# Three pairs' normalising products from VectorE to GpSimd, with a reordered broadcast and reordered weight pieces

## The chip, the core and the metric

The kernel runs on one core of a Trainium2 chip. The core has TensorE (PE in the profile; PEld is its weight load), VectorE (DVE), ScalarE (ACT), GpSimd (POOL) and SyncE (SP), which here only issues DMAs. Each engine works off its own queue in order and waits for the others through semaphores. The metric is the device time of one execution in microseconds; lower is better.

## What is computed

Attention over 4 batches of 8 heads with 576 tokens and 64 numbers per head, then a convolutional gated feed-forward layer on the joined heads:

```python
q_rot, k_rot = rotate(q), rotate(k)            # rotary embedding
scores = 1/sqrt(64) * q_rot @ k_rot.T
scores = scores - max(scores, axis=-1)
attn = exp(scores)
attn = attn / (sum(attn, axis=-1) + 1e-09)     # the normalising factor
x = (attn @ v) -> (B, 576, 512)
h = maximum(x @ w_in, 0)                       # 512 -> 1024
conv_out = 3-tap depthwise convolution of h along the tokens
out = (h * sigmoid(conv_out)) @ w_out          # 1024 -> 512
```

The weights arrive as 64-bit floats and are turned into 32-bit ones on the chip.

## The kernel before

Two heads make a pair; there are 16 pairs, four to a batch, and each takes 5 steps of the plan: pair p has its first scores in step 5p. A step holds one block of 128 query rows: scores on TensorE into PSUM (`sp`, line 259 and 285), the row maxima on VectorE (`negm`, line 267), the exponentials on ScalarE (`st`, line 271), the turning of the exponentials on TensorE (`tp`, line 319), their evacuation on ScalarE (`pt`, line 198). Five steps later the pair's product with v is made on TensorE (`emit_E`, line 396) and put into `xn` by ScalarE (line 406).

The order is written out by hand: `at(n, rank, fn)` puts a piece of work into step n, and within a step the lower rank comes first. Each engine's queue is what this order leaves on it. The steps below 26 (`WIDE`) are the first part: the pairs 0 to 5 start there and the weights are converted in between. From step 26 on TensorE also does the feed-forward layer (first matmul in line 453 for batch 0, line 463 for the others, second in line 575 and 555), and PSUM and SBUF are shared out anew.

What the change touches:

- **Rope.** GpSimd rotates q and k (lines 189 and 192, six products and three sums for each of q and k) in the raw tiles `rq` and `rk`, of which there is one each. The q of pair 4 is rotated in step 14, of pair 5 in step 19, of pair 6 in step 24, each followed by its k. VectorE then turns `rq` into `qT` (line 232) and `rk` into `kT` (line 235); only after that can SP load the next pair's q or k.
- **The normalising factor.** `emit_rinv` (VectorE, line 365 to 367) makes the reciprocals of the sums; SP writes them to DRAM (`rd`, line 370), and `emit_rb` loads them back spread over the partitions with three DMAs (`rb`, lines 376 to 378). There is one `rb` buffer: the next pair's broadcast has to wait for this pair's last product.
- **The product.** `norm` (line 414) multiplies `xn` by `rb`, two halves per pair. For batch 0 (pairs 0 to 3) the result goes to `xr`, which the first feed-forward matmul reads in step 26 and after. The steps of the two halves are 10 and 11 for pair 0, 15 and 16 for pair 1, 20 and 21 for pair 2, 24 and 25 for pair 3.
- **Weight pieces.** `WPIECES` lists 16 pieces of 128 rows and 512 columns (or the like). The first 12 are converted in the first part: an Abs on ScalarE (line 602), four operations on VectorE (lines 605, 611, 616, 621). A piece of w_in ends there, as `wr`. A piece of w_out lands in a scratch tile `wf`, ScalarE rounds it to `wouth` (line 688), and GpSimd takes the rest in four subtractions (`woutl`, line 685). In the list the eight pieces of w_in come first, then four of w_out.

The scratch tiles `wf` lie in memory that is given back at step 26; the convolution's `c` tiles (line 478, ScalarE) come to lie there.

Of the kernel before, what the change touches and what calls it, by code (L numbers as in the profile page):

```python
# [12 lines left out]
ALU = mybir.AluOpType  # L13
# [7 lines left out]
def attention_moe_kernel(ctx, tc, q, k, v, w_in, conv_w, w_out, tab, tabx, out):  # L21
    nc = tc.nc
# [5 lines left out]
    NK = DM // 128  # L28
    NF = DFF // 128
    HS = S // 2  # L30
    XW = HS + 2
# [341 lines left out]
    def emit_rb(p):  # L373
        fl = rds.pop(p).rearrange("(o t) n -> o (t n)", o=1)
        rbt = rb[p] = p1.tile([128, S], F32, tag="rb", name="rb")
        nc.sync.dma_start(out=rbt[0:64, :], in_=fl[:, 0:S].to_broadcast([64, S]))
        nc.sync.dma_start(out=rbt[64:128, 0:512], in_=fl[:, 640:1152].to_broadcast([64, 512]))
        nc.sync.dma_start(out=rbt[64:128, 512:S], in_=fl[:, 576:640].to_broadcast([64, 64]))
# [11 lines left out]
    def emit_E(p, j, a=0, n=XW):  # L390
        b, hp = divmod(p, NPB)
        xp = m_tile()[:, 0:n] if "m" in psum else spare(n)
        o = (S - XW) * j
        for i in range(5):
            for h in range(2):
                nc.tensor.matmul(  # L396
                    out=xp[64 * h:64 * h + 64, :],
                    lhsT=vmain[p][:, h, i, :] if i < 4 else vrem[p % 2][:, h, :],
                    rhs=pt[:, 2 * i + h if i < 4 else 8, o + a:o + a + n],
                    start=(i == 0),  # L400
                    stop=(i == 4),
                )
        if a == 0:
            xns[p, j] = p2.tile([128, XW], F32, tag="xn", name="xn", bufs=4)
        xn = xns[p, j]
        after(lambda: nc.scalar.activation(out=xn[:, a:a + n], in_=xp, func=AF.Copy))

        def norm():
            if plain(2 * b):
                dst = xraw[hp, j] = xtra.tile([128, XW], F32, tag="x", name="xr")  # L410
            else:
                xslot[b, hp, j] = free_slots.pop(0)
                dst = xn
            nc.vector.tensor_tensor(out=dst, in0=xn, in1=rb[p][:, o:o + XW], op=ALU.mult)

        def high():
            nc.scalar.activation(out=x_at(xslot[b, hp, j], 0), in_=xn, func=AF.Copy)  # L417

        def low():
            sl = xslot[b, hp, j]  # L420
            nc.gpsimd.tensor_tensor(out=x_at(sl, 1), in0=xn, in1=x_at(sl, 0).bitcast(F32), op=ALU.subtract)  # L421

        def both():
            norm()
            if not plain(2 * b):
                defer(1, lambda: (high(), low()))

        norms[p, j] = both
# [198 lines left out]
    def bits(i):  # L627
# [2 lines left out]
        return struct.unpack("<f", struct.pack("<I", i))[0]  # L630

    stage = {}
    WPIECES = [(w_in, None, None, kk, 1, c) for c in (0, 512) for kk in range(NK)] + [
        (w_out, wouth, woutl, f, 1, 0) for f in range(NF // 2)
    ] + [(w_out, wouth, woutl, f, 2, c) for c in (0, 256) for f in range(NF // 2, NF, 2)]

    def load_w(i):
        src, _, _, kk, rows, c = WPIECES[i]
# [107 lines left out]
    def at(n, rank, fn):  # L746
        plan.setdefault(n, []).append((rank, len(plan.get(n, [])), fn))

    def emit():
        with tc.manual_schedule(engines=engines):  # L750
# [34 lines left out]
            for p in range(NP):  # L785
                n = STEPS * p
                for s in range(STEPS):
                    m = n + s
                    first = m < WIDE
                    if m:  # L790
                        at(m - 1 if first else m, 0.5 if first else 0, lambda p=p, s=s: emit_S(p, s))
                    at(m, 0.2, lambda p=p, s=s: go(reds, (p, s)))
                    at(m, 0.3 if first else 1.5, lambda p=p, s=s: go(exps, (p, s)))
                    for h in range(2 if s < 4 else 1):
                        at(m + 1, 0 if m + 1 < WIDE else 1, lambda p=p, s=s, h=h: emit_T(p, s, h))
                if n + 4 < WIDE:
                    for i in range(4):
                        at(n + 1 + i, 2, lambda p=p, i=i: emit_Trem(p, i))
                else:
                    for i in range(4):  # L800
                        at(n + 1 + i, 1.1, lambda p=p, i=i: emit_Trem(p, i))
                if n + 8 < WIDE:
                    for i in range(4):
                        at(n + 5 + i, 4, lambda p=p, i=i: emit_E(p, i // 2, XW // 2 * (i % 2), XW // 2))
                else:
                    for i in range(2):
                        m = n + 5 + (i if n + 5 < WIDE else 0)
                        at(m, 4 if m < WIDE else 10, lambda p=p, i=i: emit_E(p, i))
                at(n + 5, 4.5, lambda p=p: emit_rinv(p))
                at(n + 5 + (n + 8 < WIDE), 17 if n + 8 < WIDE else 4.6, lambda p=p: emit_rb(p))  # L810
                for j in range(2):
                    at(n + NORM.get(p, 8 if n + 8 < WIDE else 7) + (j if p <= WIDE // STEPS else 0), 1.7 + j, lambda p=p, j=j: norms.pop((p, j))())
            whole, done = sum(c for c, _ in wsteps), 0
            for i, (c, u) in enumerate(wsteps):
                at(1 + int((WIDE - 2) * done / whole) if i else 0, 0.4, u)
# [105 lines left out]
```

## Time and profile before

| what | us |
|---|---|
| median of 3 runs | 473.69 (473.57 to 474.65) |
| the profiled execution | 474.58 |
| its span (first to last instruction) | 472.8 |
| TensorE busy | 456.9 (97%) |
| VectorE busy | 352.8 (75%) |
| ScalarE busy | 327.8 (69%) |
| GpSimd busy | 292.6 (62%) |

A row of the timeline has the start and the length of a group of equal instructions in microseconds from the span's start, the engine, the line, the operation with its tiles (out<-in), how many they are, and in brackets how long the engine stood idle before them and what ended that. A row by stretch has the busy time of each engine in that stretch, with the number of instructions. The granted TensorE clock is at its upper level in every stretch.

### The profile page before, as it was taken

Reading aid. Unit: us, or ns where it says so; the run is one execution under the profiler, and the core shown is the slowest. Engines: PE = TensorE matmul, PEld = TensorE weight load, DVE = VectorE, ACT = ScalarE, POOL = GpSimd, SP = SyncE. Lnnn points to the kernel's source line nnn. Section 1 sums busy time; section 2 is a strip of 40 time slices with the busy share of each in tenths; the row PEclk is TensorE's granted clock in tenths of the full one; section 3 lists DMA queues with packets and bytes.
Section 4 is the critical chain, followed back from the end, with each engine's and each line's share of the span. In section 5 each row is a group of like instructions: output and inputs, shape, how many; then the busy total and the mean of one; then the engine's idle time right before and its main releaser. Section 6 shows DMA issues by size and latency. Waiting matters only on the chain.

```text
span 472.8 us, 12261 instructions
## 1 busy us (share of the span) xinstructions
PE 456.9 (97%) x4563; PEld 358.2 (76%) x4563; DVE 352.8 (75%) x642; ACT 327.8 (69%) x942; POOL 292.6 (62%) x474
## 2 busy tenths in 40 slices
PE   8789999899999999999999999999999999999997
PEld 8355666556666877778787979888797878899886
DVE  4799999976999897678687786866765747468921
ACT  2789889887898877869596868868686854244400
POOL 2967884998689796997939392929430332243610
PEclk9999999999999999999999999999999999999999
DMA  9898778363571714126161717143010000100011
GB/s 230 202 214 198 161 176 191 91 155 72 121 150 50 138 37 100 40 58 118 38 139 38 139 37 134 41 90 88 27 49 28 24 27 0 46 23 24 0 68 44
DMA packets 103695, 42.63 MB, mean 90 GB/s; under 512 B 94524, under 2 KB 97876, under 8 KB 103636
## 3 DMA queue, kind: packets, MB, share of 16 engines
q1 hardware_dynamic: 103184, 41.50, 38.4%
q8 instruction: 36, 0.59, 0.5%
q10 hardware_dynamic: 452, 0.35, 0.2%
q14 instruction: 23, 0.19, 0.1%
HBM read 37.04 MB, written 4.79 MB: 88 GB/s over the span
## 4 chain that ended last, share of the span: by engine, by line
PE 76%; DVE 7%; ACT 7%; POOL 5%; DMA 2%; issue 1%; SPq 0%; DVEq 0%; POOLq 0%; ACTq 0%
PE sp L259 12%; PE pm L396 11%; PE mt L555 11%; PE pm L575 10%; PE pm L463 9%; PE mt L463 7%; PE tp L319 6%; PE pm L453 5%; ACT st L271 3%; DVE negm L267 3%; PE sp L396 2%; POOL rk L189 2%; ACT pt L198 2%; PE tp L764 1%; POOL woutl L685 1%
## 5 line engine op out<-in xcount | busy, mean ns | idle before, releaser
L267 DVE TENSOR_REDUCE negm<-sp 128x1 f32<-128x576 f32 x144 | 102.4, 747 | 27.7 <-PE sp L259 20.1
L271 ACT ACTIVATE st<-sp,negm 128x576 f32<-128x576 f32 x128 | 94.0, 742 | 26.6 <-DVE negm L267 22.4
L259 PE MATMUL sp<-kT,qT 64*128 64x288 f32 (+4 forms) x556 | 94.2, 449 | 0.7 <-ACT kT L198 0.7
L198 ACT ACTIVATE pt<-tp 128x512 f32<-128x512 f32 (+3 forms) x176 | 84.7, 535 | 4.4 <-PE tp L319 3.8
L484 DVE SCALAR_TENSOR_TENSOR c<-rr,cw,c 128x288 f32<-128x288 f32 x128 | 78.9, 616 | 4.2
L502 POOL TENSOR_TENSOR gm<-c,gm 128x288 fp32r<-128x288 f32 (+4 forms) x72 | 46.1, 645 | 48.9 <-ACT gm L501 48.7
L189 POOL TENSOR_TENSOR rq<-rq,tabt 128x192 f32<-128x192 f32 x90 | 59.6, 695 | 18.5 <-DMA rq<-q 14.3
L189 POOL TENSOR_TENSOR rk<-rk,tabt 128x192 f32<-128x192 f32 x90 | 59.1, 689 | 7.3 <-DMA rk<-k 5.4
L259 PEld LDWEIGHTS sp<-kT,qT 64*128 64x128 f32 (+1 forms) x556 | 44.4, 174 | 22.6 <-issue 9.8
L319 PEld LDWEIGHTS tp<-idf,st 64*128 64x128 f32 x1024 | 41.3, 138 | 21.3 <-ACT st L271 9.2
L319 PE MATMUL tp<-idf,st 64*128 64x64 f32 x1024 | 47.2, 226 | 5.9 <-ACT st L271 5.2
L396 PE MATMUL pm<-pt,vm 128*64 128x290 f32 x368 | 49.7, 411 | 0.2 <-ACT pt L198 0.2
L575 PE MATMUL pm<-wouth,gm 64*128 64x256 f32 x512 | 49.6, 284 | 0.0
L493 DVE SCALAR_TENSOR_TENSOR c<-c,rr 128x288 f32<-128x288 f32 x64 | 37.6, 608 | 9.5 <-ACT c L490 9.3
L482 DVE TENSOR_SCALAR c<-rr,cw 128x288 f32<-128x288 f32 x56 | 24.4, 436 | 22.7 <-ACT rr L474 22.4
L575 PEld LDWEIGHTS pm<-wouth,gm 64*128 64x128 f32 x512 | 41.0, 185 | 0.0
L421 POOL TENSOR_TENSOR xT<-xn,xT 128x290 fp32r<-128x290 f32 x18 | 15.8, 877 | 37.1 <-ACT xT L417 37.1
L396 PEld LDWEIGHTS pm<-pt,vm 128*64 128x64 f32 x368 | 25.5, 136 | 17.4 <-ACT pt L198 0.6
L463 PE MATMUL pm<-xT,wh 128*128 128x290 f32 x176 | 37.0, 302 | 0.0
L575 PE MATMUL pm<-woutl,gm 64*128 64x256 f32 x256 | 36.4, 278 | 0.0
L490 ACT ACTIVATE c<-c 128x288 f32<-128x288 f32 x64 | 28.4, 444 | 11.4 <-DVE c L484 11.4
L453 PE MATMUL pm<-xr,wr 128*128 128x290 f32 x128 | 34.5, 417 | 0.0
(135 smaller groups left out, 974.9 us busy)
## 6 DMA issues: line engine op xcount, KB each, us to landing
rq<-q SPq DMA_DIRECT2D x60, 144.0 KB
rk<-k SPq DMA_DIRECT2D x60, 144.0 KB
w<-moe_w_in SPq DMA_DIRECT2D x8, 512.0 KB
vm<-v SPq DMA_DIRECT2D x32, 128.0 KB
rb<-rd SPq DMA_DIRECT2D x16, 144.0 KB
out<-oh SPq DMA_DIRECT2D x18, 128.0 KB
rb<-rd SPq DMA_DIRECT2D x16, 128.0 KB
w<-moe_w_out SPq DMA_DIRECT2D x4, 512.0 KB
```

What stands on the lines that cost most here:

```text
L189: nc.gpsimd.tensor_tensor(out=y, in0=y, in1=tabt[:, a:a + 3], op=ALU.mult)
L198: nc.scalar.activation(out=out, in_=in_, func=AF.Copy, scale=1.0 if sc is None else sc)
L259: nc.tensor.matmul(out=out, lhsT=qt[64 * h:64 * h + 64, c], rhs=kt[64 * h:64 * h + 64, a:a + n], start=True, stop=True)
L267: reds.setdefault((p, s), []).append(lambda: nc.vector.tensor_reduce(out=nm, in_=sc, axis=AX.XY if len(sc.shape) == 3 else AX.X, op=ALU.ma ...
L271: lambda: nc.scalar.activation(out=dst, in_=sc, func=AF.Exp, bias=nm, scale=1.0, accum_out=sm)
L319: nc.tensor.transpose(ps[r][:, 64 * k:64 * k + 64], x[i], idf[i, i])
L396: nc.tensor.matmul(out=xp[64 * h:64 * h + 64, :], lhsT=vmain[p][:, h, i, :] if i < 4 else vrem[p % 2][:, h, :], rhs=pt[:, 2 * i + h if i < ...
L453: nc.tensor.matmul(out=ps[:, 0:XW], lhsT=raws[kk, half][:, gs], rhs=xraw[kk, j], start=(kk == 0), stop=(kk == NK - 1))
L463: nc.tensor.matmul(out=ps[:, 0:XW], lhsT=w, rhs=x_at(xs, e), start=(i == 0), stop=(i == n - 1))
L484: nc.vector.scalar_tensor_tensor(out=c, in0=r[:, j + e:j + e + HS], scalar=cw[:, 8 * e + f:8 * e + f + 1], in1=c, op0=ALU.mult, op1=ALU.add,)
L555: nc.tensor.matmul(out=ops[tt][:, 0:width], lhsT=g_tile(tt, f, e), rhs=w[:, f, cols], start=(f == 0 and i == 0), stop=(f == NF - 1 and i = ...
L575: nc.tensor.matmul(out=ps[r][:, 0:256], lhsT=g_tile(tt, f, e)[rows], rhs=w[rows, f, cols], start=(f == 0 and i == 0), stop=(f == NF - 1 an ...
```

## The change

The products of pairs 0, 1 and 2 (line 414, now 415) are made by GpSimd in place of VectorE. Pair 3's products stay on VectorE; its second one goes from step 25 to step 26. In step 21 pair 3's broadcast gets rank 15 in place of 17, so that SP issues it ahead of pair 6's q, which has rank 16. In `WPIECES` the four early pieces of w_out come between the two halves of w_in.

```diff
-            nc.vector.tensor_tensor(out=dst, in0=xn, in1=rb[p][:, o:o + XW], op=ALU.mult)
+            eng = nc.gpsimd if p < 3 else nc.vector
+            eng.tensor_tensor(out=dst, in0=xn, in1=rb[p][:, o:o + XW], op=ALU.mult)
...
-    WPIECES = [(w_in, None, None, kk, 1, c) for c in (0, 512) for kk in range(NK)] + [
+    WPIECES = [(w_in, None, None, kk, 1, 0) for kk in range(NK)] + [
         (w_out, wouth, woutl, f, 1, 0) for f in range(NF // 2)
-    ] + [(w_out, wouth, woutl, f, 2, c) for c in (0, 256) for f in range(NF // 2, NF, 2)]
+    ] + [(w_in, None, None, kk, 1, 512) for kk in range(NK)] + [(w_out, wouth, woutl, f, 2, c) for c in (0, 256) for f in range(NF // 2, NF, 2)]
...
-                at(n + 5 + (n + 8 < WIDE), 17 if n + 8 < WIDE else 4.6, lambda p=p: emit_rb(p))
+                at(n + 5 + (n + 8 < WIDE), 15 if n + 10 == WIDE - 1 else 17 if n + 8 < WIDE else 4.6, lambda p=p: emit_rb(p))
                 for j in range(2):
-                    at(n + NORM.get(p, 8 if n + 8 < WIDE else 7) + (j if p <= WIDE // STEPS else 0), 1.7 + j, lambda p=p, j=j: norms.pop((p, j))())
+                    at(n + NORM.get(p, 8 if n + 8 < WIDE else 7) + (2 * j if n + 10 == WIDE - 1 else j if p <= WIDE // STEPS else 0), 1.7 + j, lambda p=p, j=j: norms.pop((p, j))())
```

GpSimd's queue before, from pair 4's q to pair 6's k (`rq`, `rk` are the ropes, `woutl` the subtractions):

```order
L189 TENSOR_TENSOR rq<-rq,tabt 128x192 x6
L192 TENSOR_TENSOR rq<-rq 128x6x32 x3
L189 TENSOR_TENSOR rk<-rk,tabt 128x192 x6
L192 TENSOR_TENSOR rk<-rk 128x6x32 x3
L685 TENSOR_TENSOR woutl<-wf,wouth 128x128 x4
L189 TENSOR_TENSOR rq<-rq,tabt 128x192 x6
L192 TENSOR_TENSOR rq<-rq 128x6x32 x3
L189 TENSOR_TENSOR rk<-rk,tabt 128x192 x6
L192 TENSOR_TENSOR rk<-rk 128x6x32 x3
L685 TENSOR_TENSOR woutl<-wf,wouth 128x128 x8
L189 TENSOR_TENSOR rq<-rq,tabt 128x192 x6
```

GpSimd's queue now, from the end of pair 3's k to the end of pair 5's k and the two products behind it:

```order
L415 TENSOR_TENSOR xr<-xn,rb 128x290
L686 TENSOR_TENSOR woutl<-wf,wouth 128x128 x4
L415 TENSOR_TENSOR xr<-xn,rb 128x290
L686 TENSOR_TENSOR woutl<-wf,wouth 128x128 x4
L189 TENSOR_TENSOR rq<-rq,tabt 128x192 x6
...
L192 TENSOR_TENSOR rk<-rk 128x6x32 x3
L686 TENSOR_TENSOR woutl<-wf,wouth 128x128 x4
L415 TENSOR_TENSOR xr<-xn,rb 128x290 x2
L686 TENSOR_TENSOR woutl<-wf,wouth 128x128 x4
...
L192 TENSOR_TENSOR rk<-rk 128x6x32 x3
L415 TENSOR_TENSOR xr<-xn,rb 128x290 x2
```

Two products and eight subtractions now stand between pair 3's k and pair 4's q, as many between pair 4's k and pair 5's q, and pair 2's two products behind pair 5's k; the subtractions behind pairs 5 and 6 are gone.

VectorE's queue now, from the first row after pair 5's `kT` (step 24) to step 27:

```order
L267 TENSOR_REDUCE negm<-sp 128x1
L622 SCALAR_TENSOR_TENSOR wr<-w_1073,wt 128x512
L415 TENSOR_TENSOR xr<-xn,rb 128x290
L267 TENSOR_REDUCE negm<-sp 128x1 x2
L365 SCALAR_TENSOR_TENSOR rvc_85<-sums 128x9
...
L267 TENSOR_REDUCE negm<-sp 128x1 x2
L606 TENSOR_SCALAR room<-room 128x512
L612 TENSOR_SCALAR room<-room 128x512
L232 STREAM_TRANSPOSE qT<-rq 128x576
L415 TENSOR_TENSOR xr<-xn,rb 128x290
L267 TENSOR_REDUCE negm<-sp 128x1 x2
```

Before, pair 3's second product stood right behind the two maxima of step 25; now it stands behind pair 6's `qT`, and the first one still stands ahead of step 25's maxima.

SP's queue now, the piece of pair 3's broadcast and pair 6's q:

```order
L370 DMA rd<-rt 9x32 x4
L376 DMA rb<-rd 64x576
L377 DMA rb<-rd 64x512
L378 DMA rb<-rd 64x64
L150 DMA rq<-q 32x18x64 x4
L645 DMA room<-moe_w_out 128x2x256
L150 DMA rk<-k 32x18x64 x4
```

Before, the four loads of `rq` stood ahead of the three of `rb`. The first of a broadcast's three DMAs waits for the last reader of the `rb` buffer, which for the broadcasts of pairs 1, 2 and 3 was VectorE and is now GpSimd.

## Rows read from the trace of the kernel before

**Rows 1.** Busy time of each engine by stretch (us; instructions), clock, DMA.
```profile
82.10:99.90 17.80, 15.52 (x190) 10.16 (x188) 17.55 (x31) 14.88 (x42) 17.80 (x29) 1.00 0.52 129
99.90:111.00 11.10, 10.32 (x95) 6.91 (x91) 5.42 (x15) 6.76 (x19) 9.72 (x18) 1.00 0.58 144
111.00:130.00 19.00, 19.00 (x164) 12.97 (x164) 17.07 (x31) 17.04 (x49) 13.63 (x22) 1.00 0.33 75
...
150.00:381.00 231.00, 230.33 (x2675) 188.17 (x2673) 171.53 (x312) 177.08 (x517) 149.54 (x247) 1.00 0.32 70
```

**Rows 2.** Tile rb: VectorE's products of pairs 0 to 3 (ns min/median/max).
```profile
L414 DVE TENSOR_TENSOR xr<-xn,rb x8: 454/705/855, 48.1 to 98.8; 128x290 f32<-128x290 f32 x8
```

**Rows 3.** Timeline of VectorE: maxima of step 22, pair 5's kT and what follows.
```profile
88.89 1.41 DVE L267 TENSOR_REDUCE negm<-sp 128x1 f32<-128x576 f32 x2
...
94.28 0.76 DVE L235 STREAM_TRANSPOSE kT<-rk 128x576 f32<-128x576 f32 x1
...
96.85 0.71 DVE L414 TENSOR_TENSOR xr<-xn,rb 128x290 f32<-128x290 f32 x1
97.49 1.41 DVE L267 TENSOR_REDUCE negm<-sp 128x1 f32<-128x576 f32 x2
```

**Rows 4.** Timeline of ScalarE: exponentials of steps 22 and 25, and a tap.
```profile
90.33 0.74 ACT L271 ACTIVATE st<-sp,negm 128x576 f32<-128x576 f32 x1 [1.76 <-DVE negm L267]
...
99.90 0.74 ACT L271 ACTIVATE st<-sp,negm 128x576 f32<-128x576 f32 x1
...
109.65 0.53 ACT L478 ACTIVATE c<-rr,cw 128x288 f32<-128x288 f32 x1 [3.41 <-POOL woutl L685]
```

**Rows 5.** Timeline of TensorE: turning after step 22's exponentials; steps 26 and 27.
```profile
91.94 0.46 PE L319 MATMUL tp<-idf,st 64*128 64x64 f32 x8 [0.26 <-ACT st L271]
...
103.40 2.22 PE L453 MATMUL pm<-xr,wr 128*128 128x290 f32 x8
...
110.65 0.39 PE L356 MATMUL pm<-idf,st 64*128 64x64 f32 x2 [0.78 <-ACT pt L198]
```

**Rows 6.** Timeline of GpSimd from pair 3's k to the last early subtractions.
```profile
55.07 2.32 POOL L192 TENSOR_TENSOR rk<-rk 128x192 f32<-128x192 f32 x3
59.34 3.80 POOL L189 TENSOR_TENSOR rq<-rq,tabt 128x192 f32<-128x192 f32 x6 [1.95 <-DVE wt L616]
...
66.14 3.87 POOL L189 TENSOR_TENSOR rk<-rk,tabt 128x192 f32<-128x192 f32 x6 [1.18 <-DVE wt L616]
69.97 1.90 POOL L192 TENSOR_TENSOR rk<-rk 128x192 f32<-128x192 f32 x3
78.07 2.48 POOL L685 TENSOR_TENSOR woutl<-wf,wouth 128x128 fp32r<-128x128 f32 x4 [6.20 <-ACT wouth L688]
80.51 4.01 POOL L189 TENSOR_TENSOR rq<-rq,tabt 128x192 f32<-128x192 f32 x6
...
90.47 2.14 POOL L192 TENSOR_TENSOR rk<-rk 128x192 f32<-128x192 f32 x3
92.57 4.68 POOL L685 TENSOR_TENSOR woutl<-wf,wouth 128x128 fp32r<-128x128 f32 x8
...
107.92 1.70 POOL L685 TENSOR_TENSOR woutl<-wf,wouth 128x128 fp32r<-128x128 f32 x4
```

**Rows 7.** Groups of GpSimd by form: subtractions as large as a product (busy us, mean ns).
```profile
L421 POOL TENSOR_TENSOR xT<-xn,xT 128x290 fp32r<-128x290 f32 x18 | 15.8, 877 | 37.1 <-ACT xT L417 37.1
```

**Rows 8.** Timeline of SP: broadcasts of pairs 3 and 5.
```profile
90.59 0.46 SPq L376 DMA_DIRECT2D rb<-rd  x1
...
91.73 0.60 SPq L378 DMA_DIRECT2D rb<-rd  x1
...
131.35 0.46 SPq L376 DMA_DIRECT2D rb<-rd  x1
```

**Rows 9.** Timeline of VectorE: the product that waited for pair 5's broadcast.
```profile
136.40 0.47 DVE L414 TENSOR_TENSOR xn<-xn,rb 128x290 f32<-128x290 f32 x1 [0.92 <-DMA rb<-rd]
```

**Rows 10.** Chain that ended last, in order of time (start, us): a load of q.
```profile
89.92 2.97 DMA rq<-q
```

## Prediction

> **What bounds the kernel now.** First the busy time by stretch [rows 1]. From 111 us on TensorE has no gap worth naming: 19.00 of 19.00 us, and 230.33 of 231 us between 150 and 381. In that part a change can gain only by letting TensorE begin sooner. Up to 100 us it is otherwise: in the last stretch of the first part VectorE is busy 17.55 and GpSimd 17.80 of 17.80 us, and TensorE 15.52. Between 99.9 and 111 us TensorE lacks 0.78 us. The rows show that loss as one wait: at 110.65 it waits 0.78 us for ScalarE [rows 5], which itself stood 3.41 us in a tap (line 478) until the last early subtraction of GpSimd was done at 109.62 [rows 4]. So the question is how much sooner TensorE's first feed-forward matmul (103.40, [rows 5]) comes, and whether the 0.78 us goes.
>
> **What the change removes.** (1) Six of VectorE's eight products of batch 0, with a median of 0.705 us [rows 2]: 6 x 0.705 = 4.2 us of VectorE. What of it lies on the path is seen where ScalarE waits for the maxima: 1.76 us ahead of the exponentials of step 22 [rows 4], which follow the maxima at 88.89 [rows 3] at once. I take 1.76 us as the most that TensorE can be ahead at step 25 by this term.
> (2) The tap's wait. Its `c` tile lies where a scratch tile of a w_out piece was, and the last piece converted is now one of w_in, which GpSimd does not touch. So no wait on GpSimd is left there, and TensorE's 0.78 us goes. Ahead of the tap's new place ScalarE has time: it waits anyhow for TensorE's product with v. I count the 0.78 us whole; at worst it is 0.
>
> **What it adds.** GpSimd gets six products. The trace has none of them on GpSimd; the nearest row is its subtraction of the same 128x290, 0.877 us on average [rows 7]. From below I take VectorE's own shortest, 0.454 us [rows 2], as no row shows GpSimd the faster of the two; from above 1.28 us, the average stretched as four subtractions beside a busy VectorE were against the last four (2.48/1.70 = 1.46, [rows 6]). I take 0.88, the row of equal shape. The Trainium skill's GPSIMD Engine Reference (4.1 Engine selection) speaks against the change: a product of two inputs belongs on VectorE, being about half as fast on GpSimd. The ratio 0.877/0.454 = 1.9 agrees with it.
>
> **The queue behind them.** GpSimd works in order, so the ropes of pairs 4 and 5 stand behind the products and the moved subtractions. Pair 3's k ends at 55.07 + 2.32 = 57.39 [rows 6], and nothing of the change lies ahead of it on GpSimd. From there the new order is:
> - two products and eight subtractions: 2 x 0.88 + 4.68 (the eight at 92.57, [rows 6]) = 6.44
> - pair 4's rope: from 59.34 to 69.97 + 1.90 = 71.87, less the wait of 1.18 inside [rows 6]: 11.35
> - again two products and eight subtractions: 6.44
> - pair 5's rope: from 80.51 to 90.47 + 2.14 = 92.61 [rows 6]: 12.10
>
> 57.39 + 6.44 + 11.35 + 6.44 + 12.10 = 93.72 us, against 92.61 before. GpSimd's waits of before (1.95, 1.18 and 6.20 us, [rows 6]) pay for nearly all of the added work, but they are used up. Pair 5's `kT` was made at 94.28 [rows 3], so the maxima of step 24 are still at about their old time or a little ahead. SP is held on the way too: the broadcast of pair 1 until pair 0's second product (57.39 + 2 x 0.88 + half of 4.68 = 61.5), that of pair 2 until about 75.18 + 2.34 + 1.76 = 79.3. Behind them stand pair 4's and pair 5's k. With some 2 us for the issues ahead and 5.05 us to land (below) these are there at 69 and 86; GpSimd comes to them at 69.4 and 87.5, half a rope after 63.83 and 81.62. So this costs nothing, though by little.
>
> **The wait that is added.** Behind pair 5's k stand pair 2's two products, which end at 93.72 + 1.76 = 95.48. Only then may SP issue pair 3's broadcast, because the one `rb` buffer is read by them; before it went out at 90.59 [rows 8]. Behind it on SP are queued pair 6's q, a weight piece, pair 6's k, v of pair 5. From the first DMA of a broadcast to its product there is one row in which the product waited for it: 131.35 to 136.40, 5.05 us [rows 8, 9]. From below: the third DMA is issued 91.73 - 90.59 = 1.14 us after the first [rows 8], and a load of q took 2.97 us from issue to its release [rows 10], together 4.11. I take 4.6, the middle. The Trainium skill's page DMA: Bandwidth & Descriptors (Anatomy of one DMA) gives a fixed 2.0 us and bytes over 436 GB/s; for the 0.13 MB of the second DMA that is an estimate of 2.3 us, so 1.14 + 2.3 = 3.4 in all. By that page the sum below would end 1.2 us lower, at 472.4; the rows are longer, and I keep to them.
>
> So pair 3's first product can start on VectorE at 95.48 + 4.6 = 100.08; before it started at 96.85 [rows 3]. It stands ahead of the maxima of step 25, and the whole score path stands behind it: product 0.45 (no GpSimd work is then ready, so the shortest of [rows 2]), both maxima 1.41 [rows 3], done at 101.94. The first exponential waits for both (88.89 + 1.41 = 90.30 and 90.33, [rows 3, 4]), so step 25's start at about 101.97; they were at 99.90 [rows 4]. The second head's turning on TensorE came 91.94 - 90.33 = 1.61 us after the first exponential's start [rows 4, 5], now 103.58; it takes 0.46 [rows 5], and the first feed-forward matmul follows at about 104.1, against 103.40: **0.7 us later**. VectorE's 1.76 us of term (1) are gone in this wait. With the 0.78 us of term (2) TensorE is 0.1 us ahead from step 27 on.
>
> The other edits: pair 3's second product leaves step 25 and waits with `qT` of pair 6 in step 26. Pair 6's q is loaded behind the broadcast, about 97.2 to 99.3, is there at about 102, and its rope ends about 107.3 (5.3 us: pair 6's q and k ran from 92.57 + 4.68 = 97.25 to 107.92, [rows 6]); the maxima behind it need step 27's scores, which TensorE makes at 108 or later. That cover is thin: each us that the rope of pair 6 is later than 108 is one of TensorE. The w_out pieces' rounding on ScalarE comes earlier by the same count; ScalarE has 14.88 of 17.80 us in the last stretch, from which it is taken away [rows 1]. Both cost nothing where they stand.
>
> The sum: 4.2 us leave VectorE, of them 1.76 could be gained; the late broadcast takes these and 0.7 more; 0.78 comes from the tap. against the profiled execution (474.58, of which 1.78 lie outside the span of 472.8 and are not touched) that makes 474.5; the median of the runs, 473.69, lies 0.9 below it, so the forecast is **473.6 us**.
>
> **Rivals.**
> (A) *The broadcast comes in time.* The sum stands on 95.48 - 57.39 = 38.1 us of unbroken GpSimd work, and its rows were measured while VectorE also made the products that now leave it. Without these, and with VectorE waiting for the ropes, GpSimd may run faster: the last four subtractions took 1.70 where four took 2.48 under load [rows 6]. From 1.3 us saved on (3%) the gain is over 0.3%; from 2.5 us on (7%) product and broadcast no longer hold up VectorE, and the 1.76 us stay: 473.69 - 1.76 - 0.78 = 471.2. Against it: in the stretch with GpSimd full, VectorE's conversions go on as before.
> (B) *GpSimd becomes the bound, slower than before.* The same 38.1 us, 6% longer (2.3 us), put pair 5's k at 96 and the first feed-forward matmul 3.0 us late; less 0.78, that is 2.2: 475.9. It decides from 4% (1.5 us) on. For it: ropes under load took 12.1 where 11.35 is reckoned, and products at 1.28 us would alone add 6 x 0.40 = 2.4 us. The Trainium skill's page SBUF — State Buffer (Who interferes with whom) has a VectorE operation with two SBUF inputs and a GpSimd one shut each other out for a whole instruction, which would lengthen both sides; VectorE's product of 0.454 to 0.855 us [rows 2] fits it.
> (C) *VectorE's products were hidden anyway*, and the broadcast is no trouble: only the tap's 0.78 us is gained, 472.9.
>
> **Chances.** What a measurement of this kernel can tell from no change is about 0.3%, 1.4 us, so 472.3 to 475.1. Forecast 0.32 and (C) 0.10 lie within it, (A) 0.35 is faster, (B) 0.23 slower. The range: the broadcast's bounds (4.11 and 5.05) are +-0.5 us, the product's lead from (A) to (B); to leave out no more than 2 in 10 it must take in (A) to a little below its 471.2 and the nearer half of (B): 470.8 to 475.4. The forecast's own range is 472.3 to 475.1. Faster 0.35, same 0.42, slower 0.23.
>
> **What would show it.** Right: GpSimd without a gap from 57 to 95 us; pair 5's k ending at 93 to 95; pair 3's first product idle ahead of it until about 100, ended by the DMA of `rb`; no wait of ScalarE in the first tap; TensorE's first feed-forward matmul within 1 us of 103.4. Wrong: a broadcast of pair 3 issued ahead of 93 us, or that product without a wait (then A); a rope of pair 6 that ends after 109 us or a first feed-forward matmul at 106 (then B).

## The result, and the profile after

| kernel | us, median | runs | ratio to before, 95% interval |
|---|---|---|---|
| before | 473.63 (472.91 to 474.65) | 4 | |
| after | 479.99 (479.2 to 480.73) | 4 | 1.0125 [1.0104, 1.0146] |

The changed kernel is slower by 6 us; the forecast was 473.6 and its range ended at 475.4. The profiled execution of after took 479.20 us (span 477.4), 4.6 more than that of before, so this is what the traces have to show. Two executions of the later experiments, of 879 and 732 us, were slow and are left out of every ratio.

Where it is lost is seen by stretch, in the columns of [rows 1]:

```profile
82.10:99.90 17.80, 15.91 (x176) 9.74 (x170) 14.57 (x30) 12.89 (x34) 11.69 (x17) 1.00 0.45 89
99.90:111.00 11.10, 7.88 (x43) 4.91 (x44) 3.77 (x11) 5.51 (x15) 9.19 (x16) 0.69 0.81 171
```

Up to 99.90 TensorE is no worse off than before (15.91 against 15.52 us). From there to 111 us TensorE lacks 3.2 us, before 0.78, and the granted clock is no longer 1.00. In finer stretches:

```profile
100.00:102.00 2.00, 0.93 (x11) 0.72 (x11) 0.06 (x1) 1.08 (x5) 0.99 (x2) 1.00 1.05 264
102.00:104.00 2.00, 0.87 (x18) 0.62 (x14) 1.36 (x2) 0.00 (x1) 2.00 (x5) 0.80 1.37 186
104.00:106.00 2.00, 0.99 (x3) 0.72 (x4) 1.18 (x2) 2.00 (x5) 2.00 (x4) 0.50 0.97 206
106.00:108.00 2.00, 2.00 (x6) 1.42 (x5) 1.12 (x2) 1.38 (x4) 1.19 (x3) 0.50 0.88 246
108.00:110.00 2.00, 2.00 (x6) 0.86 (x6) 0.00 (x0) 0.41 (x1) 2.00 (x4) 0.50 0.18 36
```

TensorE works 2.79 of 6 us from 100 to 106, and from about 103 to 110 its clock is at the lower of its two levels (0.50, that is 1.2 GHz).

GpSimd (timeline, answering to [rows 6]) was done sooner than reckoned. Two products took 0.80 and 0.70 us, pair 5's k ended at 91.9, and pair 2's products right behind it at 93.79. It was not faster, though: its new queue began at 54.53 and not at 57.39, and from there to the end of pair 5's k it took 37.4 us (36.3 reckoned), of which it waited 1.90 for pair 4's k. Of the earlier begin, 1.5 us are there at pair 2's k already, ahead of the first moved product (33.11 against 34.59), so it is not all owed to the products. After pair 2's products GpSimd stood idle for pair 6's q:

```profile
54.53 0.80 POOL L415 TENSOR_TENSOR xr<-xn,rb 128x290 f32<-128x290 f32 x1
...
57.63 0.70 POOL L415 TENSOR_TENSOR xr<-xn,rb 128x290 f32<-128x290 f32 x1
...
68.09 4.16 POOL L189 TENSOR_TENSOR rk<-rk,tabt 128x192 f32<-128x192 f32 x6 [1.90 <-DMA rk<-k]
...
91.87 1.92 POOL L415 TENSOR_TENSOR xr<-xn,rb 128x290 f32<-128x290 f32 x2
101.00 3.33 POOL L189 TENSOR_TENSOR rq<-rq,tabt 128x192 f32<-128x192 f32 x6 [7.22 <-DMA rq<-q]
```

The chain that ended last, in order of time (start, us, what), tells the rest: pair 2's products on GpSimd, SP's issues behind them, the load of a w_out piece, and only then ScalarE and TensorE.

```profile
91.91 1.89 POOL xr L415 x2
93.80 0.02 issue
93.81 0.46 SPq L376
...
97.84 6.13 DMA room<-moe_w_out
103.98 0.02 issue
104.00 0.02 ACT room L603
104.02 0.54 issue
104.57 0.40 ACT xn L406
104.97 0.04 issue
105.01 0.36 PE pm L356
105.38 4.16 PE pm L454 x8
```

`room` is the scratch tile of the first of the four pieces that are converted from step 25 on. Its load stands in step 22, behind the broadcast of pair 3. Before it was issued at 92.36 and read on ScalarE at 101.50 without a wait (rows of SP and ScalarE, before):

```profile
92.36 0.59 SPq L644 DMA_DIRECT2D room<-moe_w_out  x1
...
101.50 0.68 ACT L602 ACTIVATE room<-room 128x512 f32<-128x512 f32 x1
```

Now it is issued at 97.84, since SP stood still until 93.81. On ScalarE its Abs stands behind step 25's exponentials and one short evacuation, ahead of `xn` and of step 26's exponentials (timeline of ScalarE, answering to [rows 4]):

```profile
99.36 0.74 ACT L271 ACTIVATE st<-sp,negm 128x576 f32<-128x576 f32 x1 [2.19 <-DVE negm L267]
...
104.00 0.66 ACT L603 ACTIVATE room<-room 128x512 f32<-128x512 f32 x1 [2.92 <-DMA room<-moe_w_out]
104.57 0.39 ACT L406 ACTIVATE xn<-tp 128x290 f32<-128x290 f32 x1
...
110.02 0.54 ACT L479 ACTIVATE c<-rr,cw 128x288 f32<-128x288 f32 x1
```

The exponentials of step 25 start at 99.36, 0.54 us ahead of before (99.90, [rows 4]), though VectorE had waited for the broadcast:

```profile
97.54 0.46 DVE L415 TENSOR_TENSOR xr<-xn,rb 128x290 f32<-128x290 f32 x1 [2.50 <-DMA rb<-rd]
```

So the score path that the prediction followed was in time. The tap (one term of the convolution) in the last ScalarE row has no wait on GpSimd any more, as forecast. On TensorE (answering to [rows 5]) the first feed-forward matmuls come 1.91 us late and take 4.23 us in place of 2.22:

```profile
105.01 0.36 PE L356 MATMUL pm<-idf,st 64*128 64x64 f32 x1 [2.15 <-ACT xn L406]
105.31 4.23 PE L454 MATMUL pm<-xr,wr 128*128 128x290 f32 x8
...
114.05 2.22 PE L454 MATMUL pm<-xr,wr 128*128 128x290 f32 x8
```

The next eight, of step 27, start at 114.05 against 110.97 before: 3.08 us late. At the end of the span it is 4.6 us.

```profile
110.97 2.22 PE L453 MATMUL pm<-xr,wr 128*128 128x290 f32 x8
```

### The profile page after: what moved, and what is told of

Read it like the earlier page. It is cut to its first block, busy times and chain, and to the rows that moved or that the text cites. A ratio compares the mean times of both kernels' runs of the same rounds, so it can differ in the third digit from the quotient of the medians.

```text
span 477.4 us, 12265 instructions
## 1 busy us (share of the span) xinstructions
PE 459.4 (96%) x4563; PEld 358.8 (75%) x4563; DVE 349.5 (73%) x636; ACT 327.9 (69%) x942; POOL 298.0 (62%) x480
## 4 chain that ended last, share of the span: by engine, by line
PE 70%; ACT 10%; DVE 7%; POOL 5%; DMA 4%; issue 2%; SPq 1%; DVEq 0%; POOLq 0%; ACTq 0%
PE sp L259 11%; PE mt L556 11%; PE pm L576 10%; PE pm L396 10%; PE pm L464 9%; PE mt L464 7%; PE tp L319 5%; PE pm L454 4%; ACT st L271 4%; ACT pt L198 3%; POOL rk L189 2%; DVE negm L267 2%; DMA rk<-k 2%; PE sp L396 2%; DVE c L485 1%
## 5 line engine op out<-in xcount | busy, mean ns | idle before, releaser
L259 PE MATMUL sp<-kT,qT 64*128 64x288 f32 (+4 forms) x556 | 95.4, 450 | 1.8 <-ACT pt L198 1.1
L485 DVE SCALAR_TENSOR_TENSOR c<-rr,cw,c 128x288 f32<-128x288 f32 x128 | 80.1, 626 | 4.2
L422 POOL TENSOR_TENSOR xT<-xn,xT 128x290 fp32r<-128x290 f32 x18 | 16.0, 890 | 37.4 <-ACT xT L418 37.4
L454 PE MATMUL pm<-xr,wr 128*128 128x290 f32 x128 | 36.5, 435 | 0.0
```

The lines of the kernel that those rows point to most:

```text
L259: nc.tensor.matmul(out=out, lhsT=qt[64 * h:64 * h + 64, c], rhs=kt[64 * h:64 * h + 64, a:a + n], start=True, stop=True)
L454: nc.tensor.matmul(out=ps[:, 0:XW], lhsT=raws[kk, half][:, gs], rhs=xraw[kk, j], start=(kk == 0), stop=(kk == NK - 1))
L485: nc.vector.scalar_tensor_tensor(out=c, in0=r[:, j + e:j + e + HS], scalar=cw[:, 8 * e + f:8 * e + f + 1], in1=c, op0=ALU.mult, op1=ALU.add,)
```

## The experiments

The theories that were tried against each other: **T1**, the single `rb` buffer holds SP behind GpSimd's products, and the weight piece behind the broadcast comes late; **T2**, GpSimd's own work is the bound; **T3**, VectorE's wait for the broadcast is the cause; **T4**, the order of the w_out pieces is; and later **T5**, pair 6's q behind the held broadcast. Ratios are to the kernel before on the same chip, with 95% intervals.

### Undoing one wait of the changed kernel

**The piece earlier**, ahead of the broadcast on SP:

```diff
-    LOADW = (22, 23, 29, 33)
+    LOADW = (20, 23, 29, 33)
```

> The changed kernel with one number moved: the load of the first w_out piece that is kept in `room` stands on SP in step 20 in place of step 22, so ahead of pair 3's broadcast and not behind it. T1 (the late piece): in the changed kernel the rounding of this piece on ScalarE waited 2.92 us for its DMA and everything behind it on ScalarE and TensorE with it; without that wait the first feed-forward matmul comes 2 to 3 us sooner (before 103.4), the granted clock stays at 1.00 around 105, and the time falls from 480.0 to 472 to 474. T2 (GpSimd's own work is the bound): GpSimd's queue is untouched, so the time stays at 479 to 480. T3 (VectorE's wait of 2.50 us for the broadcast is the cause): that wait stays, so 478 to 480.

Measured 476.02, ratio 1.0037 [1.0012, 1.0061]: by the ratios (1.0125 and 1.0037) about 4.2 us of the loss are gone; the time is 2 us above what T1 had expected. The first feed-forward matmul comes at 103.04 at full clock (timeline of TensorE), but GpSimd's wait stays (timeline of GpSimd):

```profile
103.04 2.22 PE L454 MATMUL pm<-xr,wr 128*128 128x290 f32 x8
...
109.51 2.22 PE L454 MATMUL pm<-xr,wr 128*128 128x290 f32 x8
```

```profile
101.79 3.70 POOL L189 TENSOR_TENSOR rq<-rq,tabt 128x192 f32<-128x192 f32 x6 [7.48 <-DMA rq<-q]
```

At 109.51 TensorE is 1.46 us ahead of before (110.97), and at the end 1.4 behind. This second loss is taken up below.

**Pair 3's products a step later**, so that VectorE's wait for the broadcast no longer stands ahead of the maxima of step 25, and **both edits** together:

```diff
-    NORM = {0: 10, 1: 10, 2: 10, 3: 9, 4: 8}
+    NORM = {0: 10, 1: 10, 2: 10, 3: 10, 4: 8}
...
-... (2 * j if n + 10 == WIDE - 1 else j if p <= WIDE // STEPS else 0) ...
+... (j if p <= WIDE // STEPS else 0) ...
```

> The changed kernel with pair 3's two products on VectorE one step later (steps 25 and 26, before 24 and 26): VectorE's 2.50 us of waiting for the broadcast no longer stand ahead of the maxima of step 25. T1 (the late piece): these maxima and exponentials come some 2 us sooner, but ScalarE still waits for the piece until about 104 and TensorE with it: 477.5 to 480, the clock still falls. T3 (VectorE's wait for the broadcast is the cause): the lead of about 2 us is kept and the time falls to 471 to 473. T2 (GpSimd's own work): 479 to 480.

> Both edits at once: the `room` piece's load in step 20, and pair 3's products in steps 25 and 26. T1: no wait for the piece, no wait for the broadcast ahead of step 25's maxima; the lead of 1.4 to 2 us that VectorE had at pairs 4 and 5 stays and the tap's 0.78 us is gained too: 470.5 to 471.5. T2 (GpSimd's own work): still above 478. T3: as with the later products alone, the early load adding nothing.

Measured 480.06 (1.0106 [1.0073, 1.0139]) for the later products, 476.18 (1.0031 [1.0015, 1.0047]) for both. In the first the exponentials of step 25 do start 1 us sooner, at 98.39, and ScalarE's wait for the piece just becomes longer (rows of ScalarE, then of TensorE):

```profile
105.83 0.67 ACT L603 ACTIVATE room<-room 128x512 f32<-128x512 f32 x1 [5.72 <-DMA room<-moe_w_out]
```

```profile
106.84 0.37 PE L356 MATMUL pm<-idf,st 64*128 64x64 f32 x1 [4.54 <-ACT xn L406]
```

T3 falls: its wait was covered by the later one, and even without the late piece it was not what was left.

**The clock.** To part the lower clock from ScalarE's lateness, matmuls with no reader were put behind one head's scores of step 25, 16 and then 8 of them:

```diff
+            if (p, s) == (5, 1):
+                for _ in range(16):
+                    nc.tensor.matmul(out=pss_[1][:, 1, 320:448], lhsT=idf, rhs=idf, start=True, stop=True)
```

> The changed kernel with 16 more 128x128 matmuls of TensorE behind one head's scores of step 25, into columns of the score tile that nobody reads; the computation is otherwise the same. They fill the stretch in which TensorE waited, and do not shorten any wait. If the fall of the granted clock (0.50 from 104 to 110) is a cause of its own worth 2.3 us, the clock stays nearer 1.00, the eight feed-forward matmuls take 2.2 us and not 4.2, and the time falls to 477 to 478.5. If the clock's fall costs nothing beyond what ScalarE's lateness costs anyhow, it stays at 480; if the extra matmuls stand in the way (about 16 x 0.2 us at most), up to 482.

> The changed kernel with 8 more 128x128 matmuls behind one head's scores of step 25, results read by nobody. With 16 the clock stayed at 1.00 and from the first feed-forward matmul to that of step 27 it took 6.47 us in place of 8.74, but the 16 themselves (3.84 us) put the first one off by 1.87 us. Eight take 1.92 us and should end before ScalarE's wait does. If the fall of the clock is a cause of its own worth 2.27 us, the time falls by 1.5 to 2.3 us, to 477.7 to 478.5, or the clock still falls with so few. If it is hidden by what else is late, it stays at 479.5 to 480.5 with the clock at 1.00.

Measured 479.66 (1.0101 [1.0073, 1.0128]) and 479.27 (1.0098 [1.0073, 1.0123]). The clock stayed at 1.00 around 105 in both. From the first feed-forward matmul to that of step 27 it is 6.47 us with 16 (107.18 to 113.65) and 6.48 with 8 (107.91 to 114.39), against 8.74 in after: the lower clock cost 2.27 us at that place. Little of it came back in the total, 0.3 and 0.7 us: the 16 put the first feed-forward matmul off by 1.87 us themselves, the result with 8 lies between the two ranges expected, and these differences are within the spread of the runs. What the clock's fall costs in the total was not settled.

### One part of the change alone

**Products only**: the kernel before, with the products of pairs 0 to 2 on GpSimd and nothing else.

```diff
-            nc.vector.tensor_tensor(out=dst, in0=xn, in1=rb[p][:, o:o + XW], op=ALU.mult)
+            (nc.gpsimd if p < 3 else nc.vector).tensor_tensor(out=dst, in0=xn, in1=rb[p][:, o:o + XW], op=ALU.mult)
```

> The kernel before with one part of the change: the products of pairs 0 to 2 on GpSimd; the order of the pieces, of pair 3's broadcast and of its products stays. T1 (the piece behind the held broadcast is late): the broadcast of pair 3 waits on SP for pair 2's products again, pair 6's q has gone ahead of it, the piece behind it comes late: 477 to 481, with a wait of ScalarE for the piece and a fall of the granted clock. T4 (the order of the w_out pieces is what costs): about 472 to 474.5. T2 (GpSimd's own work is the bound): 477 to 481 too, but with the ropes of pairs 5 and 6 themselves ending 2 us or more later than before (92.6 and 107.9).

Measured 476.17, ratio 1.0035 [1.0015, 1.0055]; below all that T1 and T2 had given. Here pair 6's q goes ahead of the broadcast, so that the piece is issued at 95.58 and ScalarE does not wait for it. But VectorE waits 2.89 us for the broadcast, TensorE 2.14 us after that, and the clock falls all the same (0.58 and 0.56 from 102 to 106):

```profile
100.98 0.99 PE L259 MATMUL sp<-kT,qT 64*128 64x288 f32 x5 [2.14 <-ACT pt L198]
...
102.92 3.60 PE L453 MATMUL pm<-xr,wr 128*128 128x290 f32 x8
```

**Pieces only**, and **all but the products** (the changed kernel with `eng = nc.vector` for every pair):

```diff
-    WPIECES = [(w_in, None, None, kk, 1, c) for c in (0, 512) for kk in range(NK)] + [
+    WPIECES = [(w_in, None, None, kk, 1, 0) for kk in range(NK)] + [
...
-    ] + [(w_out, wouth, woutl, f, 2, c) ...]
+    ] + [(w_in, None, None, kk, 1, 512) for kk in range(NK)] + [(w_out, wouth, woutl, f, 2, c) ...]
```

> The kernel before with one part of the change: the w_out pieces between the halves of w_in. T1, and the prediction's term of 0.78 us: the tap no longer waits for GpSimd (3.41 us on ScalarE, 0.78 us of TensorE), 472.9 to 473.5. T4 (the order of the pieces is what costs): 476 to 480.

> The changed kernel with all products on VectorE again: only the order of the pieces, of pair 3's broadcast and of its second product stays changed. T1: nothing holds the broadcast on SP, the piece lands in time, the clock stays at 1.00: 472 to 473.8. T4 (the pieces' order): 476 to 480. If 1.5 us or more are lost here too, the loss that was left with the early load of the piece (476.0 against 474.2) comes from the moved pieces or products and not from GpSimd.

Measured 473.96 (0.9989 [0.9974, 1.0003]) and 474.96 (1.0008 [0.9991, 1.0024]). Both lie above what T1 had given and below T4, which falls. With the pieces alone TensorE needs 6.47 us from the first feed-forward matmul to that of step 27, before 7.57: the tap's wait was worth 1.10 us there and about 0.5 in the median, which the interval does not quite part from nothing. Nothing is lost without the products.

**The late piece alone**: the kernel before, with the `room` load one step later.

```diff
-    LOADW = (22, 23, 29, 33)
+    LOADW = (23, 23, 29, 33)
```

> The kernel before with one number changed: the load of the first `room` piece stands in step 23, behind pair 6's k on SP, in place of step 22; it is then issued at about 97.7, where the changed kernel issued it (97.84), and nothing else moves. T1 (the late piece is the cause): ScalarE waits some 2 to 3 us for it ahead of the exponentials of step 26, TensorE's first feed-forward matmul comes at about 105, the granted clock falls: 476.5 to 480. T2, T3, T4: 473.5 to 474.5, as before.

Measured 474.54, ratio 1.0005 [0.9992, 1.0018]: T1's expectation was wrong. ScalarE did wait for the piece (1.83 us, until 103.21), and the first feed-forward matmul came 1.03 us late. But in this kernel the tap behind it still waits for GpSimd, and that wait shrank by as much, from 3.41 [rows 4] to 2.30 us (rows of ScalarE, then TensorE):

```profile
103.21 0.66 ACT L602 ACTIVATE room<-room 128x512 f32<-128x512 f32 x1 [1.83 <-DMA room<-moe_w_out]
...
109.41 0.54 ACT L478 ACTIVATE c<-rr,cw 128x288 f32<-128x288 f32 x1 [2.30 <-POOL woutl L685]
```

```profile
104.43 2.22 PE L453 MATMUL pm<-xr,wr 128*128 128x290 f32 x8
...
110.91 1.49 PE L453 MATMUL pm<-xr,wr 128*128 128x290 f32 x5
```

Step 27 starts at 110.91 against 110.97, and the clock stayed at 1.00. So a late piece is not enough: it costs where no other wait covers it and where it is late enough, as in after (104.00, TensorE idle 2.15 us) and unlike here (1.07 us).

### Taking away what holds SP

**A second `rb` buffer** in the changed kernel, so that the broadcast of pair 3 need not wait for pair 2's products:

```diff
-        rbt = rb[p] = p1.tile([128, S], F32, tag="rb", name="rb")
+        rbt = rb[p] = p1.tile([128, S], F32, tag="rb", name="rb", bufs=2)
```

> The changed kernel with a second `rb` buffer, so that SP need not wait for pair 2's products on GpSimd before it issues pair 3's broadcast; the work and its order on every engine stay. T1 (the held SP is the cause): the broadcast goes out by 91, the piece and pair 6's q with it, no wait of ScalarE for the piece, the clock stays at 1.00, and the time falls from 480 to 472.5 to 475. T2 (GpSimd's own work is the bound): 478 to 480. If the fast part is gone but 1.5 us are still lost, as with the early load alone (476.0), then what is left is not from SP's wait.

> The changed kernel with a second `rb` buffer once more, beside the two others on the same chip: 471.5 to 472.5 by the earlier runs, a ratio to the kernel before of 0.993 to 0.995.

Measured 471.99 (0.9936 [0.9916, 0.9956]) and again 471.42 (0.9934 [0.9909, 0.9959]), better than T1 had expected: not only is the loss gone, the kernel is 3 us faster than before. T2 falls with it, since GpSimd's work is the same. SP (first run) issues the broadcast 8.8 us sooner than in after and the piece 7.8 us sooner; TensorE's first feed-forward matmul is at 101.20:

```profile
85.01 0.46 SPq L376 DMA_DIRECT2D rb<-rd  x1
...
87.10 2.92 SPq L150 DMA_DIRECT2D rq<-q  x4
90.06 0.50 SPq L645 DMA_DIRECT2D room<-moe_w_out  x1
```

```profile
101.20 2.22 PE L454 MATMUL pm<-xr,wr 128*128 128x290 f32 x8
...
107.67 2.22 PE L454 MATMUL pm<-xr,wr 128*128 128x290 f32 x8
```

To see whose gain that is, the buffer was also given to the kernel before, and to the changed kernel with all products on VectorE (the same diff in each):

> The kernel before with a second `rb` buffer alone. In the kernel before the broadcast of pair 3 was issued behind pair 6's q at 90.59 without a wait on the buffer that the trace shows as late. If the gain of the changed kernel with two buffers (471.99 against 474.80) belongs to the buffer and not to the change: 471.5 to 473. If the buffer only takes away what the products on GpSimd bring (T1): 473.8 to 475, as before.

> The changed kernel with a second `rb` buffer and all products on VectorE again: against the changed kernel with two buffers it differs by the six products alone. If VectorE's six products are worth up to the 1.76 us that the prediction read from ScalarE's wait, this one is 1 to 2 us slower: 473 to 474.2. If they were hidden (rival C): the same, 471.8 to 472.5.

Measured 474.85 (1.0007 [0.9986, 1.0028]) and 475.00 (1.0009 [0.9993, 1.0026]). The buffer alone brings nothing; with it the six products on GpSimd bring 475.00 - 471.42 = 3.6 us (by the intervals give or take 1.4), which neither range of the second expectation had.

**Two pairs only**: pieces reordered, products of pairs 0 and 1 on GpSimd (`p < 2` in the diff of products only), one buffer.

> The kernel before with the w_out pieces between w_in's halves and the products of pairs 0 and 1 alone on GpSimd: pair 2's products stay on VectorE, so pair 3's broadcast is not held by GpSimd, and pair 6's q goes ahead of it. The new order of the pieces alone gave 473.96 against 474.53. T1 with T5 (the loss is only in what is held behind the broadcast): 472.5 to 474, the clock at 1.00, a lead of VectorE of 1 us or more at pair 5. T2 (products on GpSimd cost by themselves): 475 to 476.5, as with all six products and the early load.

Measured 474.43 (0.9988 [0.9974, 1.0002]): no loss, but no more than the pieces alone. That lies between what T1 with T5 and what T2 had given. Pair 2's products are back on VectorE, and ScalarE again waits 1.76 us at step 22.

The traces suggest why four moved products bring nothing here. The broadcast of pair 1 is held as well, until pair 0's products on GpSimd are done. In after it goes out at 58.35, 0.02 us after the second of them; pair 4's k behind it comes late, and GpSimd waits 1.90 us for it (here 1.77). From pair 4's turned q to pair 5's VectorE takes 19.3 us in after and 19.4 here, 19.0 or more in every traced kernel with one buffer, the new order of the pieces and products on GpSimd, 18.1 in before, and 16.9 to 17.5 with two buffers and the products on GpSimd. So some 1.5 to 2 us of VectorE's lead are lost ahead of pair 3's broadcast. This is read from the traces and was not tried by itself; with the products alone, in the old order of the pieces, the stretch takes 17.6 us although GpSimd waits 3.22 us for that k.

### The rest of the loss

**Pair 6's q first again**, with the early piece; the broadcast is still held:

```diff
-    LOADW = (22, 23, 29, 33)
+    LOADW = (20, 23, 29, 33)
...
-                at(..., 15 if n + 10 == WIDE - 1 else 17 if n + 8 < WIDE else 4.6, lambda p=p: emit_rb(p))
+                at(..., 17 if n + 8 < WIDE else 4.6, lambda p=p: emit_rb(p))
```

> The changed kernel with the `room` piece's load in step 20 and pair 3's broadcast behind pair 6's q again, as in the kernel before; the broadcast is still held by GpSimd. With the early load alone 1.75 us were still lost; there GpSimd stood 7.48 us waiting for pair 6's q, ran its ropes up to 4 us late, and they then lay beside VectorE's full stretch around 118 to 130, whose 15 rows took 12.16 us in place of 9.56. T5 (pair 6's q behind the held broadcast is the rest of the loss): GpSimd begins pair 6's q by 97, VectorE's stretch shrinks to under 11 us, and the time is 472 to 473.8. If the rest comes from the products themselves: 475.5 to 476.5.

> The changed kernel with the early load of the piece and pair 3's products in steps 25 and 26, for its trace: 476.2 as measured, no better than the early load alone, though VectorE no longer waits for the broadcast ahead of step 25's maxima. If pair 6's q behind the held broadcast sets the rest (T5), the exponentials of step 25 start by 98.5 (1 us sooner than with the early load alone), but GpSimd still stands idle 7 us until about 101.8, VectorE waits for its rope at about 107 as before, and the lead is gone by 130.

Measured 475.03, ratio 1.0006 [0.9987, 1.0025], so 1.5 us less loss than with the early piece alone (1.0037), just at the edge of what the two intervals can part, and 1.2 us above what T5 had expected. GpSimd begins pair 6's q at 93.93. The second kernel is that of both edits again, for its trace (one run, 477.94, late by 1.5 us already at pair 5, so only its order is read): its exponentials of step 25 have no wait, and still GpSimd is idle 7.55 us ahead of pair 6's q, and VectorE 3.24 us for that q's rope.

How a late q costs time 15 us later is seen in VectorE's stretch from pair 4's first product to the turned reciprocals of pair 5, 15 rows of the timeline. By stretch, columns as in [rows 1], of before and of after with the early piece:

```profile
118.67:128.23 9.56, 9.56 (x80) 6.24 (x78) 9.24 (x19) 8.58 (x25) 5.01 (x10) 1.00 0.65 149
```

```profile
117.53:129.69 12.16, 12.16 (x106) 8.26 (x103) 11.55 (x20) 9.49 (x27) 12.16 (x20) 1.00 0.47 118
```

GpSimd's ropes of pair 7 come later there and fill the whole stretch, and the same rows of VectorE take 2.6 us more. To try that by itself, the kernel before got seven operations on GpSimd, whose result nobody reads, ahead of pair 7's k:

```diff
+        if (p, part) == (7, "k"):
+            dm = p1.tile([128, 3, 64], F32, tag="dm", name="dm")
+            nc.gpsimd.memset(dm, 0.0)
+            for _ in range(6):
+                nc.gpsimd.tensor_tensor(out=dm, in0=dm, in1=dm, op=ALU.mult)
```

> The kernel before with seven extra GpSimd operations (a fill and six products of 128x192 on a tile that nobody else reads) in the 4.55 us in which GpSimd waited for pair 7's k, 120.25 to 124.80; the computation is otherwise the same. There VectorE's 15 rows from 118.67 to 128.23 took 9.56 us, while in the changed kernel with the early load of the piece, with GpSimd busy throughout, they took 12.16. If GpSimd's work beside it is what lengthens them: 10.6 to 12 us, and 474.5 to 476 in all (VectorE has about 1.5 us to spare there). If the length has another cause: 9.4 to 9.8 us and the time of before, 473.6 to 474.8.

Measured 475.28, ratio 1.0022 [1.0006, 1.0038], and the stretch:

```profile
117.33:128.20 10.87, 10.87 (x107) 7.34 (x102) 10.40 (x20) 9.22 (x27) 10.40 (x19) 1.00 0.56 132
```

GpSimd is 5.39 us busier, VectorE's rows are 1.31 us longer, the kernel is 1 us slower; both are within what the first reading had given. The single rows show which ones suffer: the product of 0.45 us takes 0.76, the two conversions of `room` 0.72 and 0.61 in place of 0.42 and 0.43, while two maxima take 1.41 in both (the product before, then with the extra work):

```profile
122.26 0.45 DVE L414 TENSOR_TENSOR xn<-xn,rb 128x290 f32<-128x290 f32 x1
...
121.57 0.76 DVE L419 TENSOR_TENSOR xn<-xn,rb 128x290 f32<-128x290 f32 x1
```

The Trainium skill's page SBUF — State Buffer (Who interferes with whom) has VectorE operations with two SBUF inputs meet GpSimd's reads on a shared port, and reductions never; product and maxima agree with it. That the late ropes cost the whole 1.5 us in this way is argued: the direction is shown here, the size is not.

**The old order with two buffers**: only the products, the pieces and the buffer are left of the change.

> The changed kernel with a second `rb` buffer, and with pair 3's broadcast and second product at their places of before: only the products of pairs 0 to 2 on GpSimd and the pieces' order are left of the change. The new place of the broadcast was to help a broadcast that is held; with two buffers nothing holds it, and pair 6's q, now ahead of it, is there 2 us sooner. If pair 6's q still counts: 470.5 to 471.5; if not: as with two buffers alone, 471.4 to 472.

Measured 471.03, ratio 0.9931 [0.9904, 0.9958]; it lies in the first range, but is not to be told from the 471.42 and 471.99 with the broadcast ahead. It is faster than before by 3.3 us, and by the ratios (1.0125 and 0.9931) some 9 us faster than after. The broadcast's new place and the later second product are of no use once the buffer is there.

## Why the prediction was wrong

**The step that failed** is in "the wait that is added". It named what is queued behind the broadcast on SP, "pair 6's q, a weight piece, pair 6's k, v of pair 5", and then followed only the broadcast and the q. The weight piece got no price. It had been 92.36 to 101.50 ahead of its reader on ScalarE, 9 us; issued 5.5 us later and then 6.13 us under way, it kept ScalarE waiting 2.92 us, ahead of `xn` and the exponentials of step 26. With the piece early the loss shrinks by 4.2 us (by the ratios). The lower clock, not foreseen at all, took 2.27 us over the matmuls where it fell; what part of the 4.2 that is, is open.

**"Both cost nothing where they stand"**: for pair 6's q this was wrong too. It was reckoned well (issue 97.2, there at 102; measured 95.65 and 101.00, rope done at 106.35), but cover was looked for only at TensorE's scores of step 27. The price, about 1.5 us by the q-first run, seems to arise later, where GpSimd's late ropes lie beside a full VectorE.

**"So this costs nothing, though by little"**, of the broadcast of pair 1 and the k of pair 4 behind it, was wrong: in after GpSimd waited 1.90 us for that k, and VectorE lost lead between pair 4 and pair 5 (19.3 us, with two buffers 16.9 to 17.5).

**The broadcast** was reckoned too late: pair 5's k ended at 91.9 (93.72), because the queue began 2.9 us sooner, pair 2's products ended at 93.79 (95.48), and from the first issue to the product it took 3.73 us (4.6, bounds 4.11 and 5.05). The reading that only one row shows a product waiting for its broadcast was wrong; the last broadcast in the trace of before gives 3.53 us (rows of SP, then VectorE):

```profile
386.92 0.45 SPq L376 DMA_DIRECT2D rb<-rd  x1
...
390.45 0.46 DVE L414 TENSOR_TENSOR xn<-xn,rb 128x290 f32<-128x290 f32 x1 [2.58 <-DMA rb<-rd]
```

The estimate of 3.4 that went by the Trainium skill's page DMA: Bandwidth & Descriptors (Anatomy of one DMA), whose fit is for DMAs that GpSimd issues, was nearer. So step 25's exponentials were ahead of before and not 2 us behind. The hold still has its price: with piece and q out of the way (1.0006) against two buffers (0.9936) it is 3.3 us, where the prediction had 2.5 (1.76 of lead and 0.7). But the second buffer frees the broadcasts of pairs 1 and 2 too, so the 3.3 us are not those of pair 3's alone.

**Term (1)** was mis-sized: the 1.76 us that ScalarE waits at step 22 were taken as the most that VectorE's 4.2 us could give. That wait hardly went with the products, it is 1.49 us in after; and two buffers show a gain of 3.6 us. In the first trace with two buffers the turning of q by VectorE is 0.4 us ahead of before at pair 3, 0.6 at pair 4, 1.25 at pair 5, 1.9 at pair 6 and 2.5 at pair 7, the lead growing from pair to pair; one wait is no upper bound for work that is removed in several steps.

**Term (2)**: the tap's wait went as forecast, and 1.10 us on TensorE's way with it, in place of 0.78. In the total no gain is shown: the three kernels with the new order of the pieces and all products on VectorE have 0.9989, 1.0008 and 1.0009.

**The cost of a product on GpSimd** was right: 0.70 to 0.96 us where 0.88 was taken and VectorE's shortest is 0.454. The Trainium skill's GPSIMD Engine Reference (4.1 Engine selection) has GpSimd about half as fast as VectorE at an operation of two inputs; these rows agree. With two buffers that slower work was still worth moving.

**Rivals.** (B) had the right sign, by a mechanism that did not occur: the end of GpSimd's queue was not late. (A)'s 471.2 is what the kernel gives as soon as the broadcast really comes in time (471.0 to 472.0), but its sum meets that by luck: it added 1.76 and 0.78, and measured are 3.6 and nothing clear of noise. (C), products hidden anyway, is refuted by the two kernels with two buffers.

**Open** are how the 1.75 us that the early piece leaves divide among the late k, the late q and VectorE's lengthened rows, the clock's share in the total, and which gaps of TensorE let the clock fall: it fell in after and with the products alone, but not with pair 6's q first, where TensorE was busy 1.06 of 2 us from 100 to 102.

## What to carry to other kernels

When the reader of a single-buffered tile moves to a slower or busier engine, the transfer that refills the tile waits for that engine, and so does everything behind it on the issuing queue: price each of those transfers against its own first reader, and first ask whether a second buffer fits. The same lateness can cost nothing or several microseconds, depending on whether another wait stands behind it. A wait that one engine shows at one place bounds neither the gain nor the loss of work that is moved in several steps.

## What the runs showed of the hardware

In after TensorE was busy 0.93 us from 100 to 102 and 0.87 us from 102 to 104; in the second of these stretches its granted clock went from 1.00 (2.4 GHz) to 0.50 (1.2 GHz). It stayed there until about 110, with TensorE busy without a gap since 105.0, and eight matmuls of 2.22 us took 4.23. VectorE's elementwise rows grow beside a busy GpSimd (0.45 to 0.76 us for a 128x290 product), its maxima do not (1.41 us for two in both). On the average one microsecond of GpSimd's work in the stretch of 118 to 128 cost VectorE 1.31/5.39 = 0.24 us.
